# Blocks of the small group taken turned from three groups, seven shared buffers for turned blocks, and another table of extra products

## The chip, the cores and the metric

One Trainium2 chip, one of its cores. The metric is device time in microseconds (us) of one execution of the kernel, inputs in HBM and output in HBM. The time of a kernel is the median of several executions; a profiled execution has its own time and, inside it, a span from the first to the last profiled instruction.

## The reference

Eight batches of 3200 rows; `u` and `v` have 256 columns, `z` has 64.

```python
scores = (1/S) * z @ z.T                   # [8, 3200, 3200], symmetric
x      = u * (maximum(scores, 0)**2 @ v)   # [8, 3200, 256]
wq, wk = x @ w_q, x @ w_k                  # [8, 3200, 64]
W_tok  = wq @ wk.T / sqrt(64)              # [8, 3200, 3200]
out    = maximum(W_tok @ x, 0) @ w_out     # [8, 3200, 256]
```

The kernel never forms `W_tok`: it computes `wk.T @ x` (64 x 256, the "heads") and multiplies `wq` by it (the "mix").

## The kernel before

**Tiles and groups.** The 3200 rows of a batch are 25 row tiles of 128. The columns of the score matrix are cut into seven groups: groups 0 to 5 of 512 columns (four row tiles each) and group 6, the small group, of 128 columns (row tile 24). `LASTG` is 6. The group's result is the sum over all 25 row tiles of (block of squared scores, turned as weights) times the rows of `v`; for a group of 512 columns that fills two PSUM banks (`acc0`, `acc1`).

**One tile, one pair.** A tile of the work list `tiles` (lines 246 to 275) is 512 columns wide: one row tile against a group of 512 columns, or four row tiles against the small group. Two tiles make a pair. The pair's scores (`scores`, 278) are computed by TensorE in two lanes, one on rows 0 to 63 of the array and one on rows 64 to 127 (the depth is 64): two products of 512 columns, or eight products of 128 columns for a pair of the small group. They land in one of three PSUM tiles. `first_stage` (297) takes them as `max(s, 0) * 4` into an SBUF tile `g`, on VectorE (line 303) or ScalarE (301); `second_stage` (308) squares `g` into `at` (fp16), on GpSimd (314) or ScalarE (312).

**Turned blocks.** The scores are symmetric. For some pairs of groups (`is_turned`, 237: neighbours, next but one, and 0 with 4, but never the small group) the block of squared scores is computed once, for the lower group, and turned for the higher one by a transposing DMA from `at` into a buffer `tt` (line 333). All DMAs but a few of the opening and one of the end are issued by SyncE (SP), in the order of the program; an issue that waits for a semaphore holds back all behind it. The buffers of `tt` are 3 for neighbours, 4 for next but one and 1 for 0 with 4, each kind in rotation (line 322). `weights` (418) hands a product the `at` tile or the turned one.

**Steps.** After a hand-written opening, a loop (from 946) goes step by step, `k` from 3 to 171. A step computes the scores of up to three new pairs (two when it also holds a mix), squares those of the step before, and runs a share of the current group's second product (line 351) over row tiles whose `at` is two steps old. With the second product go extra products: keys and heads of an earlier batch or group ("k"), the projection by `w_out` ("p"), or a mix ("m"). Rules say which step takes which, and a table `chosen` (843) overrides them for some values of `k`. `heading` (983) says how many of the step's score pairs stand ahead of the second product, the rest stand at shares of its length. A step that begins a group without an extra product puts all three pairs ahead. The second products run in the same two lanes, each lane on one PSUM bank; half way the lanes change banks and wait for each other (`swap_after`, 403). The second product of the small group fills one half of each of the two banks and needs no change of banks.

**Between groups.** When a group closes, `gate` (469) reads its two banks: ScalarE copies the upper (488), VectorE multiplies the lower by `u` (489), GpSimd multiplies the upper (491). The next group's first product into a bank waits for these reads. The result `x_sb` is turned by DMA (`turn_x`, 500), projected to keys (`projections_out`, 526) and turned again into `kx` (533), which the heads of a later step read as weights. An ending written out by hand follows the loop.

Of the kernel before, what the change touches and what calls it, by code (L numbers as in the profile page):

```python
# [9 lines left out]
FP16 = mybir.dt.float16  # L10
FP32 = mybir.dt.float32
# [5 lines left out]
def kernel(  # L17
# [12 lines left out]
    B, S, D = u.shape  # L30
    dqk = z.shape[2]
    dh = moe_w_q.shape[1]
    P = 128
    NT = S // P
# [3 lines left out]
    starts = [sum(widths[:i]) for i in range(len(widths))]  # L38
    NG = len(widths)
# [24 lines left out]
    ptt = ctx.enter_context(tc.tile_pool(name="ptt", bufs=1))  # L64
    psml = ctx.enter_context(tc.tile_pool(name="psml", bufs=2))
# [25 lines left out]
    zT, vs, us, xs, xTs, qks, ks, hacc, hss, rts, zds = ({} for _ in range(11))  # L91
# [143 lines left out]
    LASTG = NG - 1  # L235

    def is_turned(gi, gj):
        return gi < gj < LASTG and (gj <= gi + FAR or (gi, gj) == (0, 4))

    def group_of(ti):  # L240
        return max(gi for gi in range(NG) if starts[gi] <= ti * P)

# [6 lines left out]
    tiles, ends = [], {}  # L249
    for b in range(B):  # L250
        for gi in range(NG):
            near = [t for t in range(NT) if is_turned(gi, group_of(t))]
            own = [
                t for t in range(NT) if t not in near and not is_turned(group_of(t), gi)
            ]
            if b == 0 and gi == 0:
                order = [t for n0, nn in ZCH for t in range(n0, n0 + nn)]
                assert sorted(order) == sorted(near + own)
            else:
                odd = len(tiles) % 2  # L260
                order, rest = own[:odd], own[odd:]
                n_, m_ = len(near) // 2, (len(rest) + 1) // 2
                at_ = sorted(
                    [((i + 0.5) / max(n_, 1), near[2 * i : 2 * i + 2]) for i in range(n_)]
                    + [((i + 0.7) / max(m_, 1), rest[2 * i : 2 * i + 2]) for i in range(m_)]
                )
                for _, two in at_:
                    order = order + two
                if rest and len(rest) % 2:
                    order.remove(rest[-1])  # L270
                    order.append(rest[-1])
            many = W // widths[gi]
            tiles += [(b, gi, order[i : i + many]) for i in range(0, len(order), many)]
            ends[b, gi] = len(tiles)
    NTILE = len(tiles)
    made, turned = {}, {}

    def scores(p0, lead=0):
# [29 lines left out]
    def second_stage(p0, g, on_act):  # L308
        at = pat.tile([P, 2 * W], FP16, tag="at", name="at")
        out = at[:].rearrange("p (a w) -> p a w", a=2)  # L310
        if on_act:
            nc.scalar.square(out=out, in_=g[:])  # L312
        else:
            nc.gpsimd.tensor_mul(out=out, in0=g[:], in1=g[:])  # L314
        blocks, turns = [], []
        for h, (b, gi, tis) in enumerate(tiles[p0 : p0 + 2]):
            for i, ti in enumerate(tis):
                made[b, gi, ti] = (at, h * W + i * widths[gi])
            gj = group_of(tis[0])
            if is_turned(gi, gj):  # L320
                blocks.append((b, gi, gj, tis[0] - starts[gj] // P, 1, h * W, (h + 1) * W))
        if len(blocks) == 2 and blocks[0][:3] == blocks[1][:3] and blocks[1][3] == blocks[0][3] + 1:
            blocks = [blocks[0][:4] + (2, blocks[0][5], blocks[1][6])]
        for b, gi, gj, n0, nn, c0, c1 in blocks:
            if (b, gi, gj) not in turned:
                bufs = {1: 3, 2: 4, 4: 1}[gj - gi]
                turned[b, gi, gj] = ptt.tile(
                    [P, 4, 4, P], FP16, tag=f"tt{gj - gi}", name=f"tt{gj - gi}", bufs=bufs
                )
            out = turned[b, gi, gj][:].rearrange("p n j t -> p (n j) t")  # L330
            turns.append(
                lambda out=out[:, 4 * n0 : 4 * (n0 + nn), :], c0=c0, c1=c1:
                nc.sync.dma_start_transpose(out=out, in_=at[:, c0:c1])
            )
        return turns
# [218 lines left out]

    def heads_out(b, gis, ps):
        if gis[0] == 0:
            hacc[b] = psml.tile([P, D], FP32, tag="ha", name="ha")
            nc.vector.tensor_copy(out=hacc[b][0:dh, :], in_=ps[0:dh, 1, 0:D])
        elif gis[-1] < LASTG:
            nc.vector.tensor_add(  # L560
                out=hacc[b][0:dh, :], in0=hacc[b][0:dh, :], in1=ps[0:dh, 1, 0:D]
            )
        else:
            heads_done(b, ps[:, 1, 0:D], spread=False)
            to_spread.append(b)
# [5 lines left out]
    def heads_done(b, part, spread=True):  # L571
        hss[b] = psml.tile([P, D], FP16, tag="hs", name="hs")
        nc.vector.tensor_add(out=hss[b][0:dh, :], in0=hacc.pop(b)[0:dh, :], in1=part[0:dh, :])
        if spread:
            nc.vector.tensor_copy(out=hss[b][dh:P, :], in_=hss[b][0:dh, :])
# [183 lines left out]
    def keys_and_heads(b, gis):  # L759
# [21 lines left out]
        def after():  # L781
            for gi, o in zip(gis, outs):
                projections_out(b, gi, o)
                turn_keys(b, gi)
            if full:
                hb, hgis = keyed.pop(0)
                heads_out(hb, hgis, ps)
                if hgis[-1] == LASTG:
                    mixed_at[0] = max(mixed_at[0], now[0] - 1)
                    todo_mix.extend((hb, i, db) for i in range(LASTG // 2) for db in range(ND))  # L790
                    side.append((side_mix, side_mix_out, hb))
            if aside:
                aside[1](aside[2], ps)
            keyed.append((b, gis))
            keyed_at[0] = now[0]
# [3 lines left out]
    def group_begun(k, b, gi):  # L799
# [40 lines left out]

    chosen = {
        20: "", 21: "p", 105: "", 106: "p", 131: "k", 132: "", 134: "", 135: "p", 153: "p",
        155: "m"
    }

    def mix_due(k):
# [12 lines left out]
    def key_due(k):  # L861
        since = k - keyed_at[0]
        if not todo_between or todo_between[0][0] > k:
            return False
        if k in chosen:
            return "k" in chosen[k]
        if len(groups) <= NG:
            return since > 1
        if left is None:
            more = len(todo_between) > 1 and todo_between[1][0] <= k  # L870
            return since > 2 and (more or not todo_proj)
        begin = k + steps - 1
        if not todo_proj and not todo_mix and begin - k < 3 and begin - keyed_at[0] > 3:
            return False
        return since > 2
# [77 lines left out]
    produced, consumed, k = 16, 6, 3  # L953
# [6 lines left out]
    while groups:  # L960
# [3 lines left out]
        n = 6  # L964
        mixing = None
        if len(groups) <= 2 and NTILE - produced <= 4 and not key_due(k):
            while todo_mix:
# [4 lines left out]
        if mix_due(k):  # L972
# [3 lines left out]
            n = 4  # L976
        n = min(n, NTILE - produced)
        pairs = list(range(produced, produced + n, 2))
# [8 lines left out]
        heading = len(pairs)  # L987
        if on_lanes:
            heading = heading - 2 * bool(keying or projecting) if begins else 1 - bool(mixing)
            if begins and keying and side: heading += 1  # L990
            heading = max(0, min(len(pairs), heading))
        between_ = pairs[heading:]
        pairs = pairs[:heading]
        fresh = [(p0, scores(p0)) for p0 in pairs]
# [28 lines left out]
        for i, x in enumerate([x for x in seconds if not x[2]]):  # L1023
            (late if i else soon).extend(second_stage(*x))
        for x in acts[:1]:
            each(second_stage(*x))
# [5 lines left out]
        b, gi = groups[0]  # L1032
# [249 lines left out]
```

## Time and profile before

| what | us |
|---|---|
| median of 3 executions | 776.46 (776.32 to 776.52) |
| the profiled execution's own time | 776.48 |
| its span | 774.5 |
| TensorE busy in the span | 764.0 |
| GpSimd, ScalarE, VectorE busy | 551.2, 559.2, 475.1 |

"PE" is TensorE's products, "PEld" its weight loads, "DVE" VectorE, "ACT" ScalarE, "POOL" GpSimd, "SPq" the queue in which SyncE issues DMAs. In a row of grouped instructions the columns after the bar are the group's busy time, the mean duration of one in ns, and the engine's idle time just before them with what ended it. Products overlap in the array, so the mean duration of one is longer than the time that it adds. In the chain of waits (the work that ended last, followed back from the end) each row is: start, duration, what.

### The profile page before, as it was taken

The page shows a single profiled execution, that of the slowest core. Times are in us where ns is not written, and L with a number is a line of the kernel's source. Part 1 is how long each engine was busy: PE and PEld are TensorE (multiplying, and loading weights), DVE is VectorE, ACT ScalarE, POOL GpSimd, SP SyncE. Part 2 cuts the span into 40 slices and gives each one's busy share as a digit, 9 for nine tenths or more (in the row PEclk, how much of TensorE's full clock was granted, in tenths as well). Part 3 has the DMA queues.
Part 4 walks back from the last instruction along what each step waited for, and adds up shares of the span by engine and source line. Part 5 has one row for each costly group of instructions (what it writes and reads, how often), then busy time and mean ns, then how long its engine had stood idle before and what let it go on. Part 6 is the DMA issues. An engine that isn't in the chain of part 4 may idle for free.

```text
span 774.5 us, 28322 instructions
## 1 busy us (share of the span) xinstructions
PE 764.0 (99%) x12542; PEld 626.4 (81%) x12542; DVE 475.1 (61%) x458; ACT 559.2 (72%) x659; POOL 551.2 (71%) x360
## 2 busy tenths in 40 slices
PE   9999999999999999999999999999999999999996
PEld 6777877888788988888887887888888888888884
DVE  7654676546665577555766457655585555766444
ACT  7666786777768786686867768858786686866565
POOL 7897897778766778666878759776678566777340
PEclk9999999999999999999999999999999999999999
DMA  8999699987999679994899968999399993987627
GB/s 166 183 190 226 166 186 195 183 197 101 241 214 200 155 179 196 231 256 130 205 180 220 250 141 190 184 243 265 96 231 174 224 231 83 240 166 188 164 65 261
DMA packets 276555, 147.04 MB, mean 190 GB/s; under 512 B 252112, under 2 KB 255696, under 8 KB 276432
## 3 DMA queue, kind: packets, MB, share of 16 engines
q1 hardware_dynamic: 275712, 143.33, 85.8%
q0 software_dynamic: 576, 1.64, 1.2%
q8 instruction: 98, 1.61, 0.9%
q10 hardware_dynamic: 144, 0.26, 0.1%
q14 instruction: 25, 0.20, 0.1%
HBM read 59.38 MB, written 26.21 MB: 111 GB/s over the span
## 4 chain that ended last, share of the span: by engine, by line
PE 95%; DVE 2%; POOL 1%; DMA 1%; issue 0%; ACT 0%; SPq 0%; DVEq 0%; POOLq 0%; ACTq 0%
PE acc L351 70%; PE sc L289 12%; PE qk L351 6%; PE fo L351 5%; PE mx L604 1%; DVE g L303 1%; POOL at L314 1%; DMA z<-in_z_dram 1%; DVE x_sb L489 1%; DVE fo L1240 0%; PE ztp L130 0%; PE xtx L581 0%; POOL zd L121 0%; PE hd L591 0%; ACT g L301 0%
## 5 line engine op out<-in xcount | busy, mean ns | idle before, releaser
L303 DVE TENSOR_SCALAR g<-sc 128x1024 f32<-128x1024 f32 x338 | 411.4, 1223 | 237.4 <-PE sc L289 221.7
L314 POOL TENSOR_TENSOR at<-g 128x1024 f16<-128x1024 f32 x236 | 444.5, 1893 | 123.0 <-DVE g L303 102.3
L351 PE MATMUL acc<-v_sb,at 64*128 64x256 f16 (+1 forms) x7387 | 478.2, 269 | 1.6 <-DVE x_sb L489 0.5
L351 PEld LDWEIGHTS <-at 64*128 64x128 f16 (+1 forms) x7387 | 368.7, 94 | 84.5 <-PE acc L351 25.0
L312 ACT ACTIVATE at<-g 128x1024 f16<-128x1024 f32 x232 | 240.7, 1055 | 19.8 <-DVE g L303 13.4
L351 PE MATMUL acc<-v_sb,tt 64*128 64x256 f16 (+1 forms) x2540 | 180.1, 269 | 0.0
L289 PE MATMUL sc<-zT 64*128 64x512 f16 (+1 forms) x1104 | 170.9, 345 | 0.8 <-ACT g L301 0.5
L301 ACT ACTIVATE g<-sc 128x1024 f32<-128x1024 f32 x130 | 133.0, 1023 | 42.5 <-PE sc L289 41.6
L351 PEld LDWEIGHTS <-tt 64*128 64x128 f16 (+1 forms) x2540 | 129.6, 94 | 15.3
L491 POOL TENSOR_TENSOR x_sb<-gt,u_sb 128x512 f16<-128x512 f32 x48 | 61.2, 1275 | 69.6 <-ACT gt L488 61.0
L625 ACT ACTIVATE rt<-mx 128x1024 f16<-128x1024 f32 x47 | 47.8, 1023 | 33.9 <-PE mx L604 33.4
L289 PEld LDWEIGHTS <-zT 64*128 64x128 f16 x1104 | 57.0, 94 | 10.8 <-issue 4.1
L488 ACT COPY gt<-acc 128x512 f32<-128x512 f32 x48 | 28.1, 586 | 47.8 <-PE acc L351 45.9
L351 PE MATMUL fo<-wo,rt 64*128 64x256 f16 (+1 forms) x688 | 58.6, 270 | 0.0
L351 PE MATMUL qk<-x_sb,kx 64*128 64x256 f16 x368 | 55.3, 269 | 0.0
L526 ACT CAST qk<-qk 128x512 f16<-128x512 f32 x47 | 27.5, 585 | 37.4 <-PE qk L351 37.4
L489 DVE TENSOR_TENSOR x_sb<-acc,u_sb 128x512 f16<-128x512 f32 x48 | 33.1, 690 | 25.8 <-PE acc L351 24.8
L351 PEld LDWEIGHTS <-rt 64*128 64x128 f16 (+1 forms) x688 | 36.2, 94 | 14.5 <-PE fo L351 5.2
L686 ACT ACTIVATE fo<-fo 128x1024 f32<-128x1024 f32 x39 | 39.9, 1024 | 4.4 <-PE fo L351 4.3
L351 PEld LDWEIGHTS <-kx 64*128 64x128 f16 (+1 forms) x386 | 35.6, 94 | 6.6 <-PE qk L351 1.7
L351 PE MATMUL qk<-xT_sb,wqk 64*128 64x512 f16 (+1 forms) x94 | 27.9, 377 | 0.0
L351 PE MATMUL qk<-xT_sb,wkq 64*128 64x512 f16 (+1 forms) x90 | 26.7, 376 | 0.0
(79 smaller groups left out, 243.3 us busy)
## 6 DMA issues: line engine op xcount, KB each, us to landing
u_sb<-in_u_dram SPq DMA_DIRECT2D x48, 512.0 KB, 5.0
out_dram<-fo SPq DMA_DIRECT2D x43, 512.0 KB, 3.8
piece<-in_v_dram SPq DMA_DIRECT2D x42, 512.0 KB, 5.0
piece<-in_z_dram SPq DMA_DIRECT2D x7, 512.0 KB, 5.1
tt<-at SPq DMA_TRANSPOSE x162, 4.7
out_dram<-fo SPq DMA_DIRECT2D x9, 256.0 KB, 2.7
piece<-in_z_dram SPq DMA_DIRECT2D x7, 288.0 KB, 4.5
u_sb<-in_u_dram SPq DMA_DIRECT2D x8, 128.0 KB, 3.3
```

Of the source, the lines that this page charges most:

```text
L289: nc.tensor.matmul(out=sc[:, h, at : at + w], lhsT=zT[b][half : half + dqk, ds(z_at(b, h) + ti * P, P)], rhs=zT[b][half : half + dqk, ds(z ...
L301: nc.scalar.activation(out=g[:], in_=sc[:], func=RELU, scale=GSCALE)
L303: nc.vector.tensor_scalar(out=g[:], in0=sc[:], scalar1=0.0, scalar2=GSCALE, op0=AOP.max, op1=AOP.mult)
L312: nc.scalar.square(out=out, in_=g[:])
L314: nc.gpsimd.tensor_mul(out=out, in0=g[:], in1=g[:])
L351: return nc.tensor.matmul(out=self.out, lhsT=self.lhsT(rows), rhs=self.rhs(rows), start=start, stop=stop)
L488: nc.scalar.copy(out=upper[:], in_=accs[1][:])
L489: nc.vector.tensor_mul(out=x[:, 0:n], in0=accs[0][:, 0:n], in1=ug[:, 0:n])
L491: nc.gpsimd.tensor_mul(out=x[:, n : 2 * n], in0=upper[:], in1=ug[:, n : 2 * n])
L526: nc.scalar.copy(out=qks[b, gi][:, 0:gw], in_=out)
L625: nc.scalar.activation(out=out, in_=ps[:], func=RELU)
L686: nc.scalar.mul(out=flat_out[:, sl], in_=part, mul=FINAL_SCALE)
```

## The change

Three edits and one bookkeeping change:

1. The small group no longer computes its scores against the row tiles of groups 3, 4 and 5 (`FOR_SMALL`). Those groups compute their block against row tile 24 anyway; it is now also turned by a transposing DMA of 128 x 512 into a buffer `ts3`, `ts4` or `ts5`. The small group's list shrinks from 25 row tiles (seven tiles of four) to 13 (four tiles), and its second product reads the other twelve as turned blocks, after its own 13.
2. The eight `tt` buffers in three rotations become seven, each with its own name. A new loop hands each turned block the buffer whose last block is read out first.
3. The table `chosen` has other entries, and a new table `heading_more` moves one score pair of step 165 behind the start of the second product.
4. `hacc` has one buffer where it had two.

```diff
+    FOR_SMALL = (3, 4, 5)
...
+            if gi == LASTG:
+                own = [t for t in own if group_of(t) not in FOR_SMALL]
...
+    tt_of, tt_free = {}, [(-1.0, n) for n in range(7)]
+    for b, gi, tis in tiles:
+        gj = group_of(tis[0])
+        if is_turned(gi, gj) and (b, gi, gj) not in tt_of:
+            lefts = [t for t in range(NT) if is_turned(group_of(t), gj)]
+            last_read = lefts.index(starts[gi] // P + 3) + 1
+            tt_free.sort()
+            tt_of[b, gi, gj] = tt_free[0][1]
+            tt_free[0] = (b * NG + gj + last_read / len(lefts), tt_of[b, gi, gj])
...
-            if is_turned(gi, gj):
+            if is_turned(gi, gj) or (gj == LASTG and gi in FOR_SMALL):
...
-            if (b, gi, gj) not in turned:
-                bufs = {1: 3, 2: 4, 4: 1}[gj - gi]
-                turned[b, gi, gj] = ptt.tile(
-                    [P, 4, 4, P], FP16, tag=f"tt{gj - gi}", name=f"tt{gj - gi}", bufs=bufs
-                )
+            if gj == LASTG:
+                turned[b, gi, gj] = ptt.tile([P, 1, 4, P], FP16, tag=f"ts{gi}", name=f"ts{gi}")
+            elif (b, gi, gj) not in turned:
+                home = tt_of[b, gi, gj]
+                turned[b, gi, gj] = ptt.tile([P, 4, 4, P], FP16, tag=f"tt{home}", name=f"tt{home}")
...
-            hacc[b] = psml.tile([P, D], FP32, tag="ha", name="ha")
+            hacc[b] = psml.tile([P, D], FP32, tag="ha", name="ha", bufs=1)
...
+    heading_more = {165: -1}
     chosen = {
-        20: "", 21: "p", 105: "", 106: "p", 131: "k", 132: "", 134: "", 135: "p", 153: "p",
-        155: "m"
+        18: "k", 19: "p", 20: "p", 21: "m", 35: "k", 36: "p", 38: "p", 101: "p", 147: "k",
+        148: "m", 149: "m", 159: "mp", 161: "p", 163: "m"
     }
...
-            heading = max(0, min(len(pairs), heading))
+            heading = max(0, min(len(pairs), heading + heading_more.get(k, 0)))
```

In the built programs the loop has 169 steps before and 165 after. The counts that differ, all others being equal:

| instruction | before | after |
|---|---|---|
| score products 64 x 128 | 224 | 128 |
| first stage on VectorE, on ScalarE | 338, 130 | 330, 126 |
| second stage on GpSimd, on ScalarE | 236, 232 | 230, 226 |
| transposing DMAs `at` to `tt` | 162 | 162 |
| transposing DMAs `at` to `ts` (128 x 512) | 0 | 24 |
| second products from `at`, `tt`, `ts` | 7387, 2540, 0 | 7187, 2552, 180 |
| output projections (line 351, `fo`) | 688 | 696 |
| keys with `wqk`, heads with `kx` | 94, 368 | 92, 364 |

The second products are eight fewer in all, and the last two rows differ, because some products run as one of full depth in one kernel and as two in lanes in the other; the work in them is the same.

## The prediction

> **What bounds the kernel now.** I read the page first: busy shares, then the chain that ended last.
>
> ```profile
> span 774.5 us, 28322 instructions
> PE 764.0 (99%) x12542; PEld 626.4 (81%) x12542; DVE 475.1 (61%) x458; ACT 559.2 (72%) x659; POOL 551.2 (71%) x360
> PE 95%; DVE 2%; POOL 1%; DMA 1%; issue 0%; ACT 0%; SPq 0%; DVEq 0%; POOLq 0%; ACTq 0%
> ```
>
> TensorE holds 95% of the chain; the other engines have a quarter to a third of the span free. Next the sums of busy time in three stretches: opening, loop, ending.
>
> ```profile
> core 0: us, PE busy (x) PEld busy (x) DVE busy (x) ACT busy (x) POOL busy (x), PEclk, DMA share, GB/s
> 0.00:12.70 12.70, 10.99 (x91) 7.40 (x93) 7.17 (x10) 8.37 (x10) 7.66 (x17) 1.00 0.84 174
> 12.70:754.60 741.90, 739.77 (x12351) 609.97 (x12348) 458.27 (x435) 540.52 (x634) 543.57 (x344) 1.00 0.89 188
> 754.60:774.50 19.90, 13.22 (x104) 8.99 (x101) 9.68 (x14) 10.36 (x16) 0.00 (x0) 0.93 0.72 260
> ```
>
> The loop is 741.9 us at full clock, TensorE busy in all but 2 of them. The change edits the loop alone; the 12.7 us ahead of it and the 19.9 behind it stay. A product less on TensorE is time saved; work less on the other engines is not. A busy TensorE can still hide waits, since the ends of products are modelled, so the chain is the better witness. Here it is at the end of batch 6, in order of time:
>
> ```profile
> 638.10 1.97 PE acc L351 x36
> 640.06 0.22 PE sc L289 x8
> 640.28 1.98 PE acc L351 x36
> 642.26 0.45 PE sc L289 x16
> 649.91 1.82 PE acc L351 x32
> 651.73 0.69 DVE x_sb L489
> ```
>
> Products follow one another without a gap: a second product of 256 columns adds 1.97/36 = 0.055 us, a narrow score product of 128 columns 0.45/16 = 0.028 (0.22/8 agrees). The one break is the last row: the first product of the next group waits 0.69 us for the gate to read its bank.
>
> **The narrow products.** 96 score products of 64 x 128 go (224 to 128), twelve pairs of the small group.
>
> ```profile
> L289 PE MATMUL sc<-zT 64*128 64x128 f16 x224 | 11.6, 216 | 0.0
> L303 DVE TENSOR_SCALAR g<-sc 128x1024 f32<-128x1024 f32 x338 | 411.4, 1223 | 237.4 <-PE sc L289 221.7 <-ACT g L301 4.3 <-PE acc L351 3.0
> L312 ACT ACTIVATE at<-g 128x1024 f16<-128x1024 f32 x232 | 240.7, 1055 | 19.8 <-DVE g L303 13.4 <-DMA tt<-at 5.4
> L314 POOL TENSOR_TENSOR at<-g 128x1024 f16<-128x1024 f32 x236 | 444.5, 1893 | 123.0 <-DVE g L303 102.3 <-issue 5.7 <-DMA u_sb<-in_u_dram 2.9
> ```
>
> At 0.028 that is 96 x 0.028 = 2.7 us. Half the second product's 0.055 gives the same, as lower end 2.6; the group's busy time, 11.6/224 = 0.052, which counts the overlap of a product's end with the next, would be an upper end of 5.0. I take 2.7, since the chain leaves no overlap in.
>
> By the Trainium skill (TensorE: Matmul & The Clock Gate, Back-to-back issue gap) a stream of loads and products of 128 columns goes at about 81 ns each in the whole array. In two lanes that would be an estimate of 0.040 and 3.9 us saved, 771 in all; the trace's 0.028 decides against it.
>
> The other engines lose twelve pairs as well: 8 x 1.22 us on VectorE, 6 x 1.06 on ScalarE's squares and 4 first stages, 6 x 1.89 on GpSimd. I cost these at nothing: VectorE sat idle 221.7 us waiting for scores. The cover is TensorE's own length; without it they would be worth at most those 11 us on GpSimd, spread over eight batches. The eight second products less and the few keys, heads and projections of another form are the same columns in half as many or twice as many products: 0, at most 8 x 0.055 = 0.4 either way.
>
> **Waits between groups.** A step that begins a group without an extra product has only its three score pairs to cover the gate:
>
> ```profile
> 592.95 0.69 DVE x_sb L489
> 164.92 0.69 DVE x_sb L489
> ```
>
> Before, five such steps follow a full group: k = 7, 10, 18, 38 and 136 (the rows are 136 and 38). After, three do: 7, 10 and 37. Step 18 now begins with keys ("k" in the table), and step 136 of old has, in the new order of steps, a projection. A beginning with an extra product covers the gate with it: 8 or 16 products ahead of the first second product, 0.4 to 0.9 us. So two waits of 0.69 go. Lane changes of the extra product give a little back; I take 1.2, ends 0 (the wait shows elsewhere) and 1.4.
>
> **The small group in two steps.** Before, batch 4's small group was split over steps 105 and 106 ("" in the table), short ones, with three pairs each to read out:
>
> ```profile
> 463.90 2.34 DVE g L303 x2
> 466.28 0.71 DVE g L303
> 467.42 1.23 DVE g L303
> ```
>
> Here TensorE runs at VectorE's pace: the chain holds 4.3 us of VectorE, in which TensorE still did most of its products. The new order does that small group in one step (103) and the following step 104 begins batch 5 with three pairs and seven row tiles, like step 42 of old, where the chain shows no such stretch. Two first stages of 1.22 against a step of 3.3 us or more fit. Gain 0.4, estimated as a third of the last row; ends 0 and 1.2.
>
> **Four steps fewer.** Each step of full groups changes lanes once:
>
> ```profile
> PEld L351 <- PE acc L351: 25.0, 104, 0.3
> ```
>
> 25.0/104 = 0.24 us of an idle weight load, most of it under running products. 4 x 0.24 = 1.0 is the upper end, 0 the lower; I take 0.3.
>
> **What is added: 24 transposing DMAs.** They cost the queue and the DMA engines, and their landing has to come in time.
>
> ```profile
> L333 SPq DMA_TRANSPOSE tt<-at x162: 1195/1444/4076, 13.4 to 724.6; - x162
> DMA to landing us min/median/max: 2.5/4.7/7.6
> SPq L333 <- ACT at L312: 39.0, 19, 12.7
> q1 hardware_dynamic: 275712, 143.33, 85.8%
> ```
>
> SP: 24 x 1.2 to 1.4 = 29 to 35 us of issue, one in each of three stages of a batch. DMA engines: the queue moves 143 MB in 85.8%; 24 x 128 KB are 3.1 MB more, 2% by bytes, and some 5% of the turned data, which go in small packets (24 of half size beside 162 `tt` and about as many shorter ones): a share of 0.92 for the loop's 0.89, by estimate. That leaves room, so I expect later landings by tenths of a us and no wait. The blocks of groups 3 and 4 have five steps or more until they are read; those of group 5 have two. For these the old trace shows the stretch, since `at` of the same pair is made there and the small group read there (batch 6, steps 146 to 148):
>
> ```profile
> 641.05 1.07 ACT L312 ACTIVATE at<-g 128x1024 f16<-128x1024 f32 x1
> 641.59 1.54 SPq L195 DMA_DIRECT2D u_sb<-in_u_dram  x1
> 646.42 1.17 SPq L533 DMA_TRANSPOSE kx<-qk  x1
> 654.16 2.07 PE acc L351 x38
> ```
>
> `at` is ready at 642.1, SP is free from 643.1 until 646.4, and the group's last four row tiles, the turned ones of group 5 in the new order, come in the last sixth of the 654.16 row, near 655.9. That leaves 13.8 us for an issue and 4.7, at most 7.6, to landing: slack of some 5 us. Cost 0; if the cover were gone, each us too late is a us for each of eight batches. In the new order the issue stands behind a small load of `u` and in batches 2 to 7 an output, ahead of the next batch's turned blocks and a `kx`.
>
> **Seven buffers for eight.** A turned block's DMA waits until its buffer's last block was read. Counting steps between that reading and the first DMA into the buffer: 2 or more before, 1 or more after (twice exactly 1: batch 2 step 52, batch 7 step 158). In program order the reading is over when that step begins; what queues behind on SP is a turned `x_sb` with several steps to spare. Cost 0, upper end a wait of one first part of a step, 1 us each time, on SP, not on TensorE. `hacc` with one buffer: the next batch's first write comes steps after the last read: 0.
>
> **A tight place that moves.** Near the end keys and heads come two steps apart:
>
> ```profile
> 676.90 0.59 ACT L526 CAST qk<-qk 128x512 f16<-128x512 f32 x1
> 679.59 2.29 SPq L533 DMA_TRANSPOSE kx<-ql  x1
> 682.71 0.61 PE qk L351 x5
> L351 PEld LDWEIGHTS <-kx 64*128 64x128 f16 x382 | 35.2, 94 | 6.6 <-PE qk L351 1.7 <-DMA kx<-ql 0.2
> ```
>
> The heads at 682.7 read what was issued at 679.6, and the trace has 0.2 us of waiting for it, so the slack is nil. After, the same pair of steps is 150 and 152; with five row tiles in each of 150 to 152 for 7, 6 and 6, and a projection in 151. Between the two keys that is 8, 8 and 2 second products less and 16 projection products more, of 0.055 each: 0.1 us shorter. I put a wait of 0.2 there, ends 0 and 1.5 (a further transfer ahead of it).
>
> **The sum**, against the profiled execution's 776.48 (the median of the runs is 776.46, so nothing is to be converted): 776.48 - 2.7 - 1.2 - 0.4 - 0.3 + 0.2 = 772.1. I round up to 772.3 for transfers that are later here and there. With all ends in favour 776.5 - 2.7 - 1.4 - 1.2 - 1.0 = 770.2; with all against and the narrow products alone, less 1.5 at the tight place, 775.3.
>
> **Rivals.**
>
> 1. *Only the products count.* The waits between groups and VectorE's pace come back at other beginnings, since the table moves which steps have extra products (steps 37, 40, 41, 103, 104 still have none). Then 776.5 - 2.7 + 0.2 = 774.0. For it: the rules are sensitive to the order of steps. Against: the waits can be counted by step, and I counted fewer. 0.15.
> 2. *The small group waits for its last turned block; slower.* One mechanism: group 5's block is issued behind an output or a load whose own wait holds SP (the row with 12.7 us is the longest such wait), so that `at` to landing is over 13.8 us; TensorE then stands in the second product of the small group, eight times. 12.7 + 7.6 - 13.8 = 6.5 us at the worst; at 1.5 on average it is 12 us and 772.3 + 12 = 784. It decides from 0.6 us per batch on (8 x 0.6 cancels the 4.4 gained). Against: SP's free 3.3 us in the row above. 0.08.
> 3. *SP and the DMA engines are the second bound.* 30 us more of issue and a share of 0.92 for 0.89 make the close deliveries late: the `kx` above, and the buffers of `at`, which a transposing DMA keeps longer (ScalarE's squares waited 5.4 us for `tt<-at`). Ten waits of 0.3 to 0.5 give 776 to 777. For it: the 0.2 above. Against: all `tt` blocks but one are read four or more steps after their issue, and that one three. 0.07.
>
> **How the numbers follow.** The forecast, 770.2 to 773.5 with 772.3, has 0.70. A measurement of this kernel can tell about 0.2% (1.6 us) from no change, so "faster" ends at 774.9. Faster: forecast and rival 1, less a little for its upper edge: 0.84. Within 0.2%: half of rival 3 and that edge: 0.07. Slower: rival 2 and a little of 3: 0.09. The range reaches from 770.4 to 774.9: it holds the forecast and rival 1.
>
> **What would show it.** In the profile after: narrow score products x128 with a busy time near 6.6; products on TensorE still follow at 0.055; the chain with `DVE x_sb` of 0.69 at three beginnings of full groups; no wait on a DMA of `ts` in the list of waits; the stretch around batch 4's small group without a run of `g` rows in the chain; DMA share of the loop near 0.92. I am wrong if PEld or PE waits for `ts` or `tt`, if SP's issues to landing grow past 7 us in the median, or if VectorE's `g` appears in the chain at steps 40 and 41 or 103 and 104.

## The result and the profile after

| kernel | median of runs, us | runs | ratio to before, 95% interval |
|---|---|---|---|
| before | 776.61 | 6 | |
| after | 772.81 (771.71 to 773.50) | 6 | 0.9941 (0.9921 to 0.9962) |
| after, a second set of runs | 771.91 (771.61 to 772.81) | 5 | 0.9942 (0.9929 to 0.9954) |

The change makes the kernel faster by 0.6%, 3.8 us by the medians of the first set and 4.7 by those of the second. The forecast was 772.3 and its range 770.4 to 774.9. The profiled execution of after took 773.23, its span 771.4.

The page of after, busy time and the chain's shares, and then the sums of three stretches in the columns of the prediction's:

```profile
PE 760.0 (99%) x12440; PEld 621.0 (81%) x12440; DVE 466.2 (60%) x450; ACT 549.8 (71%) x649; POOL 540.2 (70%) x354
PE 97%; DVE 1%; issue 0%; DMA 0%; ACT 0%; POOL 0%; SPq 0%; ACTq 0%; DVEq 0%
```

```profile
core 0: us, PE busy (x) PEld busy (x) DVE busy (x) ACT busy (x) POOL busy (x), PEclk, DMA share, GB/s
0.00:12.70 12.70, 10.77 (x89) 7.30 (x89) 6.90 (x10) 8.10 (x10) 7.53 (x16) 1.00 0.88 181
12.70:751.50 738.80, 736.11 (x12253) 604.86 (x12252) 449.59 (x427) 531.37 (x625) 532.72 (x338) 1.00 0.94 193
751.50:771.40 19.90, 13.08 (x103) 8.88 (x100) 9.70 (x14) 10.35 (x16) 0.00 (x0) 0.92 0.72 259
```

The opening and the ending are cut off here at the lengths that they had before (by the steps below, the opening is 0.3 us longer in this execution and 0.4 shorter in a second one); with these cuts the loop is 3.1 us shorter, still at full clock and still TensorE's. VectorE, ScalarE and GpSimd each lose 9 to 11 us of work, more than the kernel gained, so that this work was hidden, as assumed. The loop's DMA share is 0.94 for the 0.92 expected, and the `tt` blocks land after 5.0 us in the median where it was 4.7.

The narrow products in the view by operation, and the new blocks `ts` in the view by tile:

```profile
L307 PE MATMUL sc<-zT 64*128 64x128 f16 x128 | 6.2, 216 | 0.0
```

```profile
L369 PEld LDWEIGHTS <-ts x180: 94/94/98, 94.7 to 751.2; 64*128 64x128 f16 x168, 128*128 128x128 f16 x12
L351 SPq DMA_TRANSPOSE ts<-at x24: 1194/1218/2601, 66.5 to 743.8; - x24
DMA to landing us min/median/max: 2.5/4.9/8.1
```

The narrow products are busy for 6.2 us (6.6 expected). The 24 issues take 1.2 us each, and the blocks land 4.9 us later in the median, far from the 7 that would have made me wrong. TensorE reads them 180 times, and neither its products nor its weight loads are among those that waited for them; the list of waits has a single 0.3 us of a weight load for a `tt`, in this execution and not in the second. To the letter that is one of the prediction's signs of being wrong; at 0.3 us it decides nothing. Rival 2 did not come.

**Where the time came from.** The steps can be measured one by one: a step's length is the time from its first product to the first of the next. From it I took what its products need at the pace at which they follow one another in these traces where nothing waits (0.0545 us for one of 64 x 256, 0.108 for 64 x 512, 0.028 for 64 x 128, double for full depth); what is left is the step's excess. The table is worked out from the traces of before, of after, and of a second profiled execution of after (span 769.8).

| us | before | after | after, second execution |
|---|---|---|---|
| products at the traces' pace | 730.14 | 727.45 | 727.45 |
| excess of step 10 | 0.70 | 1.51 | 0.61 |
| excess of group 5 of batch 0 (step 18 on) | 0.61 | 0.10 | 0.10 |
| excess of group 2 of batch 6 (step 136 of old on) | 0.58 | 0.08 | 0.08 |
| small group of batch 4 and the group behind it | 1.09 | 0.65 | 0.65 |
| excess of all other steps | 8.76 | 8.60 | 8.63 |
| loop | 741.88 | 738.38 | 737.52 |

Rows two to four of the excess are the prediction's steps, one after the other; row one is a wait that it did not have. It stands out in the timelines of ScalarE and TensorE, after first and then its second execution:

```profile
37.16 1.06 ACT L330 ACTIVATE at<-g 128x1024 f16<-128x1024 f32 x1 [5.07 <-DMA tt<-at]
38.12 1.01 ACT L319 ACTIVATE g<-sc 128x1024 f32<-128x1024 f32 x1
39.18 0.61 PE L307 MATMUL sc<-zT 64*128 64x512 f16 x4 [1.05 <-ACT g L319]
```

```profile
35.64 1.06 ACT L330 ACTIVATE at<-g 128x1024 f16<-128x1024 f32 x1 [4.17 <-DMA tt<-at]
36.60 1.00 ACT L319 ACTIVATE g<-sc 128x1024 f32<-128x1024 f32 x1
37.66 0.61 PE L307 MATMUL sc<-zT 64*128 64x512 f16 x4 [0.15 <-ACT g L319]
```

The square wants a free `at` buffer, which a transposing DMA still reads. It holds ScalarE, the first stage behind it comes late, and TensorE's next scores wait for the PSUM tile that this stage empties: 1.05 us in one execution, 0.15 in the other. Before has the same wait (0.24 us behind a square that waited 4.27), the first block for the small group is issued at 66.5 us, and the kernel with the new buffers alone has 0.56 us of excess at step 10. So neither the blocks nor the buffers are seen to cause it; over the traces of all kernels with 11 `at` buffers that excess lies between 0.56 and 1.51 us.

**The waits between groups.** Before, at step 18 (chain of waits, then TensorE's timeline), and after at the same step:

```profile
75.99 1.79 PE acc L351 x32
77.83 0.59 ACT gt L488
78.46 2.22 PE acc L351 x36
```

```profile
77.57 0.82 PE L289 MATMUL sc<-zT 64*128 64x512 f16 x12
78.46 1.77 PE L351 MATMUL acc<-v_sb,at 64*128 64x256 f16 x28
```

```profile
76.16 2.64 PE acc L369 x48
78.80 0.22 PE sc L307 x2
79.02 0.43 PE qk L369 x5
```

The keys now stand where the gate's row stood. But the row of 0.59 or 0.69 is not what it costs: while the gate reads, TensorE computes the step's twelve score products. Step 18 exceeds its products by 0.56 us without keys and by 0.04 with them; the whole group's excess falls by 0.51.

The chain of after has the gate's row at seven small groups, 92.67 and 649.20 being the first and the last, where before had it at four:

```profile
92.67 0.69 DVE x_sb L507
462.58 0.69 DVE x_sb L507
463.32 2.90 PE acc L369 x50
649.20 0.70 DVE x_sb L507
```

```profile
649.94 0.83 PE L369 MATMUL acc<-v_sb,at 64*128 64x256 f16 x12 [0.16 <-DVE x_sb L507]
```

TensorE's own timeline has 0.16 us idle at the last of them. A small group's step in one piece has an excess of 0.29 to 0.33 us with the row; before, it had 0.22 without it in batch 1 and 0.04 in batch 2, where keys stood ahead that have gone. So these two small groups together cost 0.33 us more than before, which lies among "all other steps". In the same stretch, 462.58 to 466, VectorE's `g` no longer appears: batch 4's small group is one step, at TensorE's pace.

### The profile page after: what moved, and what is told of

The parts are those of the page before. It is cut to its first block, busy times and chain, and to the rows that moved or that the text cites. A ratio compares the mean times of both kernels' runs of the same rounds, so it can differ in the third digit from the quotient of the medians.

```text
span 771.4 us, 28170 instructions
## 1 busy us (share of the span) xinstructions
PE 760.0 (99%) x12440; PEld 621.0 (81%) x12440; DVE 466.2 (60%) x450; ACT 549.8 (71%) x649; POOL 540.2 (70%) x354
## 4 chain that ended last, share of the span: by engine, by line
PE 97%; DVE 1%; issue 0%; DMA 0%; ACT 0%; POOL 0%; SPq 0%; ACTq 0%; DVEq 0%
PE acc L369 71%; PE sc L307 12%; PE qk L369 6%; PE fo L369 5%; PE mx L622 1%; DVE x_sb L507 1%; DMA z<-in_z_dram 0%; DVE g L321 0%; PE ztp L130 0%; PE xtx L599 0%; PE hd L609 0%; ACT g L319 0%; ACT fo L1263 0%; DVE fo L1259 0%; PE qq L369 0%
## 5 line engine op out<-in xcount | busy, mean ns | idle before, releaser
L321 DVE TENSOR_SCALAR g<-sc 128x1024 f32<-128x1024 f32 x330 | 401.7, 1223 | 243.2 <-PE sc L307 223.1
L332 POOL TENSOR_TENSOR at<-g 128x1024 f16<-128x1024 f32 x230 | 433.6, 1895 | 136.0 <-DVE g L321 113.5
L369 PE MATMUL acc<-v_sb,at 64*128 64x256 f16 (+1 forms) x7187 | 462.9, 269 | 1.5 <-DVE x_sb L507 0.5
L369 PEld LDWEIGHTS <-at 64*128 64x128 f16 (+1 forms) x7187 | 355.8, 94 | 86.8 <-PE acc L369 24.6
L330 ACT ACTIVATE at<-g 128x1024 f16<-128x1024 f32 x226 | 234.9, 1055 | 15.8 <-DMA tt<-at 8.7
L369 PE MATMUL acc<-v_sb,tt 64*128 64x256 f16 x2552 | 180.7, 269 | 0.0
L307 PE MATMUL sc<-zT 64*128 64x512 f16 (+1 forms) x1008 | 165.9, 357 | 1.4 <-ACT g L319 1.3
L369 PEld LDWEIGHTS <-tt 64*128 64x128 f16 x2552 | 130.6, 94 | 15.2
L307 PEld LDWEIGHTS <-zT 64*128 64x128 f16 x1008 | 52.4, 94 | 10.8 <-issue 4.2
L369 PE MATMUL qk<-x_sb,kx 64*128 64x256 f16 (+1 forms) x364 | 54.7, 269 | 0.0
```

The costliest lines, as they stand in the source:

```text
L307: nc.tensor.matmul(out=sc[:, h, at : at + w], lhsT=zT[b][half : half + dqk, ds(z_at(b, h) + ti * P, P)], rhs=zT[b][half : half + dqk, ds(z ...
L321: nc.vector.tensor_scalar(out=g[:], in0=sc[:], scalar1=0.0, scalar2=GSCALE, op0=AOP.max, op1=AOP.mult)
L369: return nc.tensor.matmul(out=self.out, lhsT=self.lhsT(rows), rhs=self.rhs(rows), start=start, stop=stop)
```

## The experiments

**Narrow products twice.** On the kernel before:

```diff
+            for _ in range(2 if w == P else 1):
-            nc.tensor.matmul(
+                nc.tensor.matmul(
...
```

> The kernel before, with each narrow score product of the small groups (64 x 128) issued twice: 224 products more, every other instruction as it was; they write what the first ones wrote. My theory (a narrow product costs 0.028 us of the path, from the chain's 0.45 us for 16): 224 x 0.028 = 6.3 us more, some 782.9 us. Rival by the group's busy time (11.6 us for 224, 0.052 each): 11.6 us more, 788.2. Rival that such products fall into gaps and cost nothing: under 2 us more. The Trainium skill (TensorE: Matmul & The Clock Gate, Back-to-back issue gap) would make it, by an estimate of 0.040 us in two lanes, 9.0 us more.

783.39 us, ratio 1.0086 (1.0068 to 1.0103): 6.5 us for 224 products by the medians, 0.029 each. The chain of this kernel, in a step of the small group:

```profile
646.73 0.89 PE sc L290 x32
647.62 0.87 PE acc L352 x16
```

0.89/32 is 0.028. My price holds to 0.001; the interval's 5.3 to 8.0 us leaves out 11.6 and 9.0. The group's busy time (20.1 us for 448) is no price: the products overlap each other and those beside them.

**The buffers alone**, on the kernel before: seven shared `tt` buffers, `hacc` with one.

```diff
+    tt_of, tt_free = {}, [(-1.0, n) for n in range(7)]
...
-                    [P, 4, 4, P], FP16, tag=f"tt{gj - gi}", name=f"tt{gj - gi}", bufs=bufs
+                turned[b, gi, gj] = ptt.tile([P, 4, 4, P], FP16, tag=f"tt{home}", name=f"tt{home}")
...
+            hacc[b] = psml.tile([P, D], FP32, tag="ha", name="ha", bufs=1)
```

> The kernel before with the seven shared buffers for turned blocks and the single buffer of the heads' sum alone; the order of steps and all products as before. My theory: no difference (within 0.5 us of the before runs, 776.3 to 777.1), and no wait of TensorE on a turned block. Rival (a transposing DMA now waits for its buffer's reader and the blocks land late): 1 us or more slower, with a wait of the weight loads on a turned block in the list of waits.

776.88 us beside 776.86, ratio 0.9995 (0.9984 to 1.0005). The blocks land in 4.7 us in the median, as before. Neither a cost nor a gain of the edit can be seen (the interval reaches from 1.2 us faster to 0.4 slower).

**The table's early entries left out**, on the kernel after:

```diff
-        18: "k", 19: "p", 20: "p", 21: "m", 35: "k", 36: "p", 38: "p", 101: "p", 147: "k",
-        148: "m", 149: "m", 159: "mp", 161: "p", 163: "m"
+        147: "k", 148: "m", 149: "m", 159: "mp", 161: "p", 163: "m"
```

> The kernel after, with the entries of the table up to step 101 left out; those from 147 on, which the last batch needs, stay. Step 18 then begins a full group without an extra product again, and other keys, heads and projections of the early steps fall where the rules put them. My theory (one wait between groups is worth 0.69 us, the table's other early entries nearly nothing): 0.7 us slower than after, some 773.5, with the gate's 0.69 in the chain at the beginning of step 18, near 92 us. Rival that the products alone count: the same as after, 772.8 or less. Rival that the table carries most of the gain: 775 or more.

773.15 us, ratio 0.9949 (0.9937 to 0.9962), within the range of after's runs (771.61 to 773.50): the measured time alone doesn't settle it. The trace has the wait of step 18 back,

```profile
78.00 0.60 ACT gt L506
78.64 2.22 PE acc L369 x36
```

at 78 us, not near 92 as I had written (the row there is the small group's). The group's excess is 0.61 for 0.10; the loop's excess is 11.72 for 10.07 in the second execution of after, of which step 10 has 0.39 and the early entries 1.26. I had expected these entries to be worth one wait and nearly nothing else: step 18 is 0.51 of it, and the rest is the sum of rises and falls in later groups (up 0.28 in group 0 of batch 4 and 0.25 in group 1 of batch 3, down 0.25 in the small group of batch 2). The largest part of the gain is not the table's: the products alone are 2.69.

**One more `at` buffer.** The memory that the buffers left holds a twelfth `at`. On the kernel after, twice, with after itself beside it the second time; and on the kernel before with the buffers of the change:

```diff
-    NAT = 11
+    NAT = 12
```

> The kernel after with 12 buffers for the squared scores (at) rather than 11; the memory for it is what the turned blocks' buffers left free. In the trace of after ScalarE's square near 37 us waits 5.07 us for an at buffer that a transposing DMA still reads, and TensorE's scores wait 1.05 us behind it. My theory (that wait goes and with it most of the spread of the runs of after, 771.7 to 773.5): 0.2 to 1.0 us faster, 771.8 to 772.6, and no wait of the squares for a transposing DMA near 37 us. Rival (the wait only moves, since the transposing DMAs are late by themselves): the same, 772.8.

> The kernel after, unchanged, beside the kernel with 12 at buffers on the same chip, to tell whether the difference of their medians (772.81 and 771.94, from two sets of runs) is one. My theory: 772.8 again, runs between 771.7 and 773.5, the square near 37 us waiting longer in some executions than in others. Rival (the two are the same kernel in time, and the medians differ by chance): the median within 0.3 us of the other's.

> The kernel with 12 at buffers, unchanged, a second time. My theory: 771.9 again, runs within 771.5 and 772.4, 0.5 us or more below the kernel after in the same set of runs. Rival: the same as after.

> The kernel before with the seven shared buffers, the single buffer of the heads' sum and 12 at buffers: what the freed memory is worth without the other parts of the change. In the trace of before the scores near 38 us wait 0.24 us behind a square that waits for an at buffer (4.27 us). My theory: 0.1 to 0.5 us below before, 776.3 to 776.7, since little of that wait reaches TensorE there. Rival (the twelfth buffer is worth the same 0.9 us in every kernel): 775.9 or less.

| kernel | median, us | ratio to before |
|---|---|---|
| after with 12 `at`, first set | 771.94 | 0.9934 (0.9920 to 0.9947) |
| after with 12 `at`, second set | 772.01 | 0.9943 (0.9931 to 0.9956) |
| after, second set | 771.91 | 0.9942 (0.9929 to 0.9954) |
| before with buffers and 12 `at` | 776.38 | 0.9996 (0.9987 to 1.0005) |

The first set fitted my theory that the wait near 37 us makes the difference; the second did not bear it out. With 12 buffers the long wait is gone; ScalarE's timeline of the second execution waits for TensorE there, and for no buffer:

```profile
34.95 1.02 ACT L319 ACTIVATE g<-sc 128x1024 f32<-128x1024 f32 x1 [2.12 <-PE sc L307]
```

The excess of step 10 is 0.56 us in all four traces with 12 buffers. But after alone gave the same median in the second set, and on the kernel before the twelfth buffer is worth nothing that can be seen, as expected. That the first set's 772.81 was higher because the wait was longer in it fits the two traces of after (1.51 and 0.61 us of excess at step 10), which are one execution of each set; more was not shown. No version here beats after.

**The blocks for the small group turned twice**, on the kernel after:

```diff
+            if gj == LASTG:
+                spare = ptt.tile([P, 1, 4, P], FP16, tag="spare", name="spare", bufs=2)
+                turns.append(
+                    lambda out=spare[:].rearrange("p n j t -> p (n j) t"), c0=c0, c1=c1:
+                    nc.sync.dma_start_transpose(out=out, in_=at[:, c0:c1])
+                )
```

> The kernel after, with each of the 24 transposing DMAs of the small group issued twice, the first time into a spare tile that nobody reads: the load that the change added to SP and the DMA engines is doubled, TensorE's program is the same. My theory (SP and the DMA engines have room): within 0.5 us of after (771.7 to 773.5 in its runs), no wait of the weight loads on a turned block beyond the 0.3 us seen in after, DMA share of the loop near 0.96. Rival 3 of the prediction (SP and the DMA engines are the second bound): 3 us or more slower than after, from 776, with issue-to-landing of the turned blocks growing past 6 us in the median.

772.49 us, ratio 0.9956 (0.9939 to 0.9973); nine of twelve runs within 771.5 to 773.6, three at 775.7 to 778.8. Runs of before reached 778.7 beside them, so that I read nothing from those three.

```profile
12.70:751.50 738.80, 737.08 (x12259) 606.83 (x12255) 449.62 (x428) 530.95 (x625) 531.80 (x338) 1.00 0.98 198
```

```profile
L357 SPq DMA_TRANSPOSE ts<-at x24: 1255/1266/2111, 63.5 to 743.7; - x24
DMA to landing us min/median/max: 2.5/4.2/7.1
```

Those are the sums of the stretch that is nearly the loop, and the view of the blocks that are read. The share of the DMA engines is 0.98, the blocks land no later (the `tt` after 4.9 us in the median), and TensorE waits for none. At the change's load, and at twice its addition, rival 3 is out.

**Group 5's block late**, on the kernel after: issued when the small group begins.

```diff
-    made, turned = {}, {}
+    made, turned, held = {}, {}, []
...
-            turns.append(
+            (held if (gi, gj) == (LASTG - 1, LASTG) else turns).append(
...
         while to_turn:
             turn_x(*to_turn.pop(0))
+        if groups[0][1] == LASTG:
+            each(held)
+            held.clear()
```

> The kernel after, with the turned block of group 5 for the small group held back: it is issued on SP when the small group begins, behind the turn of group 5's x_sb, and not with its second stage two steps earlier. This prices rival 2. In the trace of after, batch 6: SP ends that turn at 652.53, so the block would be issued near 652.6 and land some 5 us or more later, near 657.5 to 658.5; TensorE reads it near 653.2. My theory (the small group's second product has no cover, what is late there falls on the end whole): 4.3 to 5.3 us in each of eight batches, 34 to 43 us slower than after, 807 to 816. Rival (TensorE finds other products to do meanwhile): under 10 us slower.

801.30 us, ratio 1.0310 (1.0292 to 1.0327): 28.5 us slower than after's first median, 3.6 per batch. The waits, the chain at batch 6 and the chain at batch 0:

```profile
PEld L369 <- DMA ts<-at: 22.0, 8, 3.2
```

```profile
671.93 1.28 POOL x_sb L509
673.22 1.24 SPq L518
674.52 2.57 DMA ts<-at
677.14 0.61 PE acc L369 x8
```

```profile
95.27 2.61 DMA ts<-at
97.92 0.61 PE acc L369 x8
...
100.52 2.52 PE acc L369 x28
```

That a late block falls on the end undiminished is shown: eight waits of the weight loads. My number for one was too high, because I took the median landing of 4.9 us. These two landed in 2.6; the DMA engines had a share of 0.01 to 0.04 in the stretches just ahead. And in batch 0 something else follows the wait: 28 products take 2.52 us, 0.090 each instead of 0.055 (see the last section).

**Four groups turned**, on the kernel after, with a table of one entry:

```diff
-    FOR_SMALL = (3, 4, 5)
+    FOR_SMALL = (2, 3, 4, 5)
...
-    heading_more = {165: -1}
-    chosen = {
...
+    heading_more = {}
+    chosen = {155: 'm'}
```

> The kernel after with group 2's blocks turned for the small group too (8 transposing DMAs more, 32 narrow score products fewer, 164 steps rather than 165), and of the table only one entry for the last batch (155: "m"). The nearest kernel is the one with the table's late entries alone, 773.15. My theory: 32 x 0.028 = 0.9 us less for the products, 0.1 for the step, and 0.4 more for a full group that begins without an extra product at step 78: some 772.5, no wait on the small group's blocks. Rival 3 (each further turned block makes deliveries late): 774 or more, with waits on turned blocks.

774.13 us, ratio 0.9959 (0.9947 to 0.9971): 1.6 us above my number, and inside rival 3's. The reason is another. Neither products nor weight loads are in its list of waits for a turned block; the chain breaks at a `kx` instead:

```profile
676.84 2.27 DMA kx<-ql
679.16 0.28 PE qk L369
```

The products at the traces' pace fell by 0.90 us as expected. But group 1 of batch 7 has an excess of 1.22 us (0.13 to 0.23 in the kernels with three groups). That is the prediction's tight place, two keys with a `kx` between them: the step that waits for it has 0.46, and the two steps behind it 0.66, whose cause was not looked into. Group 4 of batch 5, now in two steps, has 0.64 for 0.08; groups 2 of batch 7 and 5 of batch 3 begin without cover and have 0.59 each. What the fourth group is worth with a table made for it was not tried.

**Step 18 bare again**, with 12 `at`:

```diff
-        18: "k", 19: "p", 20: "p", 21: "m", 35: "k", 36: "p", 38: "p", 101: "p", 147: "k",
+        19: "p", 20: "k", 21: "m", 35: "k", 36: "p", 38: "p", 101: "p", 147: "k",
```

> The kernel with 12 at buffers (771.94), with the keys of step 18 moved to step 20, so that the full group at step 18 begins without an extra product; the rest of the table stays. My theory, by the length of step 18 in the traces (0.64 to 0.66 us over the pace of its products without an extra product, some 0.2 with keys): 0.45 us slower, 772.4. Rival as the prediction had it (the wait is worth the chain's 0.69): 0.7 slower, 772.6. Rival that it is hidden: 771.9.

772.30 us, ratio 0.9936 (0.9925 to 0.9948): 0.3 above the two sets with 12 `at`, and not to be told from them by the ratios. By the trace the group's excess is 0.59 for 0.10, so 0.49 us for one wait, and there is 0.2 more in the next group but one (group 0 of batch 1), which now begins without keys too.

## Why the prediction was right

The sum took 4.4 us off the profiled execution of before, and 4.2 after rounding. The second execution of after is 4.7 us shorter in its span (774.5 to 769.8) and 4.36 in its loop; the first is 3.1 and 3.5, because of step 10 and a slower opening.

| term | predicted | loop, before to second execution of after |
|---|---|---|
| narrow products | 2.7 | 2.69 (96 fewer at the traces' pace); 0.029 each when doubled |
| waits between groups | 1.2 | 1.01 (0.51 + 0.50) |
| small group of batch 4 in one step | 0.4 | 0.44 |
| four steps fewer, tight place near the end | 0.3 - 0.2 | 0.13 (all other steps; batch 7's group 1 has 0.16 for 0.28) |
| 24 DMAs, seven buffers, `hacc` | 0 | 0: no wait on `ts`; buffers alone 0.9995 |
| not in the prediction | | 0.09 (step 10), -0.81 in the first execution |

Point by point. The narrow products were priced from the chain, and the experiment chose the chain's 0.028 over busy time and over the estimate that the prediction worked out from the figure of the Trainium skill (TensorE: Matmul & The Clock Gate, Back-to-back issue gap). Of the waits the number that go, two, was right; the price of 0.69 from the chain was too high by more than a third, 0.5 being what a group loses. I read the row at 651.73 as the first product of a full group standing for 0.69 us; it is the small group's, and such a row turned out to stand for 0.16 us of idle time. The count of "three beginnings" holds for full groups (24.52, the scores at 39.18, a gate's row at 165.84), not for the rows of the chain. Batch 4's small group did what the prediction said; this was read from the traces and not tried alone. The DMAs were hidden as said, with the share two points above the estimate.

The term for four steps fewer is not shown. It was priced by the weight loads that wait at the change of lanes, and that row of after, with the heads' weight loads of its second execution, is now

```profile
PEld L369 <- PE acc L369: 24.6, 103, 0.3
L369 PEld LDWEIGHTS <-kx 64*128 64x128 f16 x374 | 34.6, 94 | 6.0 <-PE qk L369 1.2 <-DMA kx<-qk 0.2
```

One such wait went, not four, and 0.4 us of idle weight loads. The 0.13 us of all other steps is the sum of many rises and falls, the 0.33 of the two small groups among them. At the tight place the second row has the 0.2 us that before had, and no more: the slack is still nil, and the 0.2 us put in as a further wait did not come. So part of the agreement is luck: errors of 0.2 in both directions cancel, and step 10, which the prediction did not have, differs by 0.9 us between two executions of one kernel.

Rival 1 fell: two waits went for good, though a third of what they gave came back at the small groups of batches 1 and 2. Rival 2's mechanism is real, shown by the held-back block, and its condition never arose; its price, one us for each us late, was too low where the wait reached 2.7 us (see the last section). Rival 3 fell with the doubled blocks. The prediction's upper end for the tight place was worth having: with four groups that transfer does stand in the chain.

## What to carry to other kernels

Price a product that is taken away by the pace of the chain, not by busy time or mean duration, since products overlap. A row of another engine in the chain between two stretches of TensorE tells which wait ended last, not what it costs: compare the whole step's length with that of a step which has cover. Extra transposes on a busy queue were free here because each block was issued two steps or more before its reading; at these loads (DMA shares of 0.94 and 0.98) that distance decided, not the load.

## What was not expected of the hardware

A stall of TensorE can cost more than its own length. In the kernel with the late block, the first products behind the wait and the granted clock of 4.1 us that begin about a us later, for batches 0, 1, 3 and 6:

```profile
97.92 0.61 PE L369 MATMUL acc<-v_sb,ts 64*128 64x256 f16 x8 [2.72 <-DMA ts<-at]
190.04 0.61 PE L369 MATMUL acc<-v_sb,ts 64*128 64x256 f16 x8 [2.74 <-DMA ts<-at]
386.57 0.61 PE L369 MATMUL acc<-v_sb,ts 64*128 64x256 f16 x8 [2.18 <-DMA ts<-at]
677.14 0.61 PE L369 MATMUL acc<-v_sb,ts 64*128 64x256 f16 x8 [1.81 <-DMA ts<-at]
```

```profile
98.90:103.00 4.10, 4.10 (x43) 2.85 (x38) 1.79 (x3) 4.10 (x6) 3.72 (x4) 0.58 0.13 27
191.00:195.10 4.10, 4.04 (x44) 2.81 (x42) 2.54 (x3) 2.96 (x4) 3.69 (x4) 0.58 0.18 36
387.50:391.60 4.10, 4.10 (x76) 3.27 (x72) 2.66 (x3) 4.10 (x6) 3.67 (x4) 1.00 0.50 163
678.10:682.20 4.10, 4.10 (x74) 3.65 (x72) 2.91 (x4) 3.88 (x6) 3.70 (x5) 1.00 0.47 157
```

In the first two stretches the mean clock is 0.58 (by the trace's record it is 0.50 for 3.41 us of them, from 98.98 and 191.14 on), 43 and 44 products run in place of 74 to 76, and the group behind has 1.5 to 1.6 us more excess. After 2.18 and 1.81 us of waiting it stays at 1.00, and so it does after 1.87 us in batch 5. Batches 2 and 4 (2.90 and 2.73 us) fell likewise, from 290.13 and 484.69 on, and batch 7 (2.87 us) from 778.24 on, in the ending. What the groups behind batches 0, 1, 2 and 4 lost makes 6.4 of the 28.5 us.

The Trainium skill (TensorE: Matmul & The Clock Gate, HAM oscillation — how this bites in real kernels) warns of idle gaps above some 3.4 us; here 2.7 was enough, and the measurement decides. A limit for the length of a wait is not shown by this. The five falls begin whole multiples of 3.413 us apart (27, 29, 57 and 86 of them), as if the clock were set at fixed times. In the 3.41 us ahead of each fall TensorE was idle for 2.2 to 2.9 us; the three shorter waits lie across such a time and leave at most 1.5 us on one side. So the idle share of a fixed stretch would explain the eight cases as well as the length of the wait does; no run here tells them apart.
